# Attention followed by a gated projection, on one core: loads of batch 1 ahead of w_out, the first output by quarters, and the front of batch 2 in its own slot

## The chip, the cores and the metric

The kernel runs on one core of one Trainium2 chip. The metric is device time in microseconds (us), as the median of the runs. The kernel before takes 264.88 us (264.41 to 265.37 in the four runs). Inside the profile the span from the first to the last instruction is about 2 us shorter than the measured time: 263.0 us for the kernel before.

The **granted clock** is the TensorE clock that the throttle allowed, as a share of full speed. A **slot** is one round of the steady state: it computes `h` of one batch while `out` of the batch before fills TensorE's gaps. **T** is the moment at which the matmuls of `s1(2)`, the first attention scores of batch 2, start in the changed kernel. A run's **state** is fast or slow, and only fast runs are compared; here "slow" also covers runs over 1.5% above the fastest run of the same kernel, at an ordinary clock.

## The reference

```python
# q, k, v: [8 batches, 8 heads, 576, 64];  p: [8, 8, 32, 64];  w_in [512, 2048], w_out [2048, 512]
def sm_attn(qq, kk, vv):
    s = scale * (qq @ kk.T);  s = s - max(s)
    a = exp(s);  a = a / (sum(a) + 1e-9)
    return a @ vv
p_packed = sm_attn(p, k, v)               # 32 summary rows for each head
out = sm_attn(q, p_packed, p_packed)
x = out, with the heads side by side      # [8 * 576, 512]
h = x @ w_in
g = h * cos(h)
return g @ w_out                          # [4608, 512] float32
```

## The kernel before

Each batch goes through a chain, its *front*: transpose k; `s1` (p with k, Exp); transpose that result (`a1T`); `pp` (times v); `ppw` (times `w_in`, in four pieces); transpose q; `s2` (q with pp, Exp); `sums2` and `normalise`. Then come `h_mm`, sixteen steps of matmul, cosine on ScalarE and product on VectorE, and `out`, sixteen matmuls for each of its four or five chunks.

Transposes of k, q and a1 are made on TensorE for the first batches (`pe_T`, `a1_pe`) and by DMA later (`xbar`, `a1_xbar`). The DMA transposes and nearly all output stores are issued from the same queue, SyncE's, in program order. Input loads are issued from GpSimd's.

```python
att_pool = ctx.enter_context(tc.tile_pool(name="att", bufs=1))   # kT, qT, a1T: one buffer each
A = ctx.enter_context(tc.tile_pool(name="psA", bufs=3, space=PSUM))
O = ctx.enter_context(tc.tile_pool(name="psO", bufs=2, space=PSUM))

def xbar(n, b):
    t = xT[n, b] = att_pool.tile([128, H * 3, TP], BF16, name=n + "T", tag=n + "T")
    nc.sync.dma_start_transpose(out=t, in_=bf[n, b].rearrange("p h x -> p (h x)"))
def a1_xbar(b): ...                       # the same for a1, on the same queue

# --- loads: all of w_out (2 MB) ahead of batch 1
# ... k 0, v 0, q 0, w_in ...
for n in range(4):
    load_w_out(n)
load("k", 1)
# ... v 1, q 1, k 2, v 2, q 2 ...

# --- first phase: h of batch 0
sums2(0, 0)
sums2(0, 1)
ppw(0, 1)                                 # its copy on ScalarE stands ahead of normalise
normalise(0)
warm(6)                                   # warm-up: matmuls whose result isn't used
dup_p(2, 16)
for fc in range(NFC):
    h_mm(0, fc)()
    # ... ppw(0, 2), ppw(0, 3), pack_p(1, 3) among them ...

# --- fronts of batches 1 AND 2, filled with out of batch 0
# ... s1(1), pp(1), s2(1), k 2 transposed, s1(2), normalise(1), a1_pe(2) ...
load("k", 3)

def slot(s, pieces, hooks): ...           # h of batch s, out of s-1, given pieces of fronts

def begin_loads(b):                       # a "gate": GpSimd reads kT, so it waits for its transpose
    G.tensor_copy(out=gate, in_=xT["k", b][0:1, 0, 0:1])
    for n, i in (("v", b), ("q", b), ("k", b + 1)):
        load(n, i)

xbar("q", 2)
xbar("k", 3)
slot(1, [..., (7, lambda: pp(2)), ...], [(8, lambda: begin_loads(3))])

for s in range(2, B):                     # steady state
    # ... s2(s), fill(8) ...
    s1(s + 1)
    xbar("q", s + 1)
    xbar("k", s + 2)
    a1_xbar(s + 1)
    # ... sums2, normalise, loads of v s+2, q s+2, k s+3 ...
    slot(s, [..., (5, lambda: pp(s + 1)), ...], [])
```

The softmax here doesn't subtract the row's maximum and nothing guards it: scores larger than these inputs give would overflow.

## Time and profile before

| | before |
|---|---|
| time, median of 4 runs | 264.88 us |
| span in the profile | 263.0 us |
| TensorE busy | 93% |
| first cosine of batch 0 | 23.61 us |
| first Exp of `s1(1)` | 41.53 us |
| slot 1 ends, `s2(2)` follows | 75.82 us |
| gate, with the loads of v 3, q 3, k 4 behind it | 68.31 us |
| `pp(3)` starts, without a wait | 91.59 us |
| `s2(3)` starts: slot 2 is over | 106.70 us |

These are from parts 1 and 2 of the page of the kernel before: busy time with its share of the span, then the span in 40 slices of 6.6 us, each digit the busy share (or the granted clock) in tenths.

```profile
PE 244.6 (93%) x2037; PEld 132.1 (50%) x2037; DVE 158.5 (60%) x248; ACT 182.7 (69%) x276; POOL 53.5 (20%) x67
...
PE   8758779998989999999999999999999999999993
...
PEclk9997999999999999999999999999999999999998
```

From slice 13 on, which begins at 79 us, TensorE is busy all the time, so time can be won only before that. The table of busy time by stretches has more detail; its columns are the stretch, its length, then for each engine busy us with its count of instructions, the granted clock, the DMA share, and GB/s.

```profile
core 0: us, PE busy (x) PEld busy (x) DVE busy (x) ACT busy (x) POOL busy (x), PEclk, DMA share, GB/s
...
93.00:101.00 8.00, 8.00 (x62) 4.31 (x61) 6.35 (x9) 5.64 (x10) 0.61 (x1) 1.00 1.22 201
101.00:106.00 5.00, 4.99 (x44) 2.61 (x42) 3.98 (x5) 3.74 (x6) 0.00 (x0) 1.00 0.65 133
```

Both rows lie in slot 2. Here TensorE is busy 12.99 of 13 us.

The timeline of ScalarE around the first cosine shows the delay that the change aims at first: start, duration, engine, line, operation, and in brackets the idle time before it and what ended it.

```profile
17.18 1.25 ACT L200 ACTIVATE lns<-psA 128x576 f32<-128x576 f32 x2
19.93 1.01 ACT L75 CAST PPW<-psA 128x1024 bf16<-128x1024 f32 x1 [1.51 <-PE psA L182]
20.84 1.26 ACT L206 ACTIVATE lns<-lns 128x576 f32<-128x576 f32 x2
22.12 1.28 ACT L225 ACT_TABLE_LOAD   x1
23.61 0.74 ACT L225 ACTIVATE cosT<-psA,pihalf 128x576 bf16<-128x576 f32 x1 [0.21 <-PE psA L221]
```

After the two Ln (L200) ScalarE waits 1.51 us for `ppw(0, 1)`, copies its result (L75), and only then runs the two Exp of `normalise` (L206).

The timeline of SyncE's queue shows the three transposes that slot 2 needs, one behind the other.

```profile
79.21 3.40 SPq L93 DMA_TRANSPOSE qT<-qbf  x1
82.79 2.96 SPq L93 DMA_TRANSPOSE kT<-kbf  x1
85.80 1.57 SPq L147 DMA_TRANSPOSE a1T<-a  x1
```

The duration is the time that the queue was held: the first ends at 82.61 us and the next starts at 82.79, that one ends at 85.75 and the last starts at 85.80. The transpose of a1 lands 3.8 us after its issue, at 89.6 us. `pp(3)`, which needs it, starts at 91.59 us without a wait.

### The profile page before, as it was taken

Reading aid. Unit: us, or ns where it says so; the run is one execution under the profiler, and the core shown is the slowest. Engines: PE = TensorE matmul, PEld = TensorE weight load, DVE = VectorE, ACT = ScalarE, POOL = GpSimd, SP = SyncE. Lnnn points to the kernel's source line nnn. Section 1 sums busy time; section 2 is a strip of 40 time slices with the busy share of each in tenths; the row PEclk is TensorE's granted clock in tenths of the full one; section 3 lists DMA queues with packets and bytes.
Section 4 is the critical chain, followed back from the end, with each engine's and each line's share of the span. In section 5 each row is a group of like instructions: output and inputs, shape, how many; then the busy total and the mean of one; then the engine's idle time right before and its main releaser. Section 6 shows DMA issues by size and latency. Waiting matters only on the chain.

```text
span 263.0 us, 5065 instructions
## 1 busy us (share of the span) xinstructions
PE 244.6 (93%) x2037; PEld 132.1 (50%) x2037; DVE 158.5 (60%) x248; ACT 182.7 (69%) x276; POOL 53.5 (20%) x67
## 2 busy tenths in 40 slices
PE   8758779998989999999999999999999999999993
PEld 3433446455534555456445644464446554565452
DVE  2446886748853787358835685378735873578110
ACT  1358882497698757987798768877897678886000
POOL 8523002440422220504050302220040000000000
PEclk9997999999999999999999999999999999999998
DMA  6999999999399899399949992899194111111232
GB/s 95 203 226 206 206 204 197 192 186 201 47 203 203 189 165 187 73 193 173 221 95 184 168 221 75 159 188 176 47 158 113 40 42 40 40 46 36 80 82 80
DMA packets 62919, 37.09 MB, mean 141 GB/s; under 512 B 35520, under 2 KB 58304, under 8 KB 62896
## 3 DMA queue, kind: packets, MB, share of 16 engines
q0 software_dynamic: 23168, 18.81, 47.1%
q1 hardware_dynamic: 39568, 17.83, 31.5%
q8 instruction: 16, 0.26, 0.4%
q10 hardware_dynamic: 160, 0.13, 0.2%
q14 instruction: 7, 0.06, 0.1%
HBM read 37.22 MB, written 9.44 MB: 177 GB/s over the span
## 4 chain that ended last, share of the span: by engine, by line
PE 66%; DMA 13%; ACT 9%; DVE 7%; issue 2%; POOL 1%; DVEq 0%; ACTq 0%; POOLq 0%
PE ot L271 39%; PE psA L221 17%; DMA kbf<-in_k_dram 7%; DMA w_in_bf<-in_moe_w_in_dram 5%; DVE gT L228 4%; ACT cosT L225 3%; PE psA L182 2%; PE psA L163 2%; DVE PPW L77 2%; ACT PPW L75 1%; ACT L438 1%; PE psA L124 1%; PE ot L260 1%; PE psA L198 1%; PE psA L102 1%
## 5 line engine op out<-in xcount | busy, mean ns | idle before, releaser
L271 PE MATMUL ot<-w_out_bf,gT 128*128 128x512 bf16 x512 | 132.1, 380 | 0.0
L225 ACT ACTIVATE cosT<-psA,pihalf 128x576 bf16<-128x576 f32 x128 | 94.0, 742 | 32.0 <-PE psA L221 30.7
L228 DVE TENSOR_TENSOR gT<-psA,cosT 128x576 bf16<-128x576 f32 x128 | 94.9, 754 | 33.7 <-ACT cosT L225 32.6
L221 PE MATMUL psA<-a2n,PPW 128*128 128x288 bf16 x512 | 83.4, 285 | 5.5 <-DVE gT L228 3.1
L221 PEld LDWEIGHTS <-PPW 128*128 128x128 bf16 x512 | 49.9, 97 | 43.0 <-issue 13.0
L271 PEld LDWEIGHTS <-gT 128*128 128x128 bf16 x512 | 47.0, 98 | 42.8 <-issue 7.1
L232 POOL COPY joint<-gT 128x512 bf16<-128x512 bf16 x16 | 9.7, 614 | 111.1 <-DVE gT L228 111.1
L208 DVE SCALAR_TENSOR_TENSOR a2n<-a2u,r,lns 128x576 bf16<-128x576 bf16 x16 | 12.4, 815 | 20.1 <-ACT lns L206 20.1
L77 DVE COPY osb<-ot 128x512 f32<-128x512 f32 (+1 forms) x19 | 12.7, 670 | 15.1 <-PE ot L271 12.0
L75 ACT COPY osb<-ot 128x512 f32<-128x512 f32 (+1 forms) x18 | 10.3, 574 | 15.0 <-PE ot L271 10.1
L77 DVE CAST PPW<-psA 128x1024 bf16<-128x1024 f32 x16 | 19.5, 1220 | 1.5 <-PE psA L182 1.2
L75 ACT CAST PPW<-psA 128x1024 bf16<-128x1024 f32 x16 | 16.1, 1005 | 2.6 <-PE psA L182 2.6
L77 POOL COPY vp<-vbf 96x3072 bf16<-96x3072 bf16 x6 | 16.5, 2749 | 1.2 <-DMA vbf<-in_v_dram 1.2
L182 PE MATMUL psA<-w_in_bf,ppT 64*32 64x512 bf16 x256 | 13.4, 393 | 2.2 <-DMA w_in_bf<-in_moe_w_in_dram 1.5
L271 PE MATMUL ot<-w_out_bf,joint 128*128 128x512 bf16 x48 | 12.9, 380 | 0.0
L190 ACT ACTIVATE a2u<-psA,rs 128x576 bf16<-128x576 f32 x16 | 11.0, 738 | 2.5 <-PE psA L124 2.4
L200 ACT ACTIVATE lns<-psA 128x576 f32<-128x576 f32 x16 | 10.5, 658 | 2.3 <-PE psA L198 2.3
L133 ACT ACTIVATE a<-psA 128x576 bf16<-128x576 f32 x16 | 10.3, 651 | 2.6 <-PE psA L124 2.6
L173 ACT CAST ppT<-psA 64x128 bf16<-64x128 f32 x16 | 4.2, 260 | 10.8 <-PE psA L102 6.5
L142 DVE RECIPROCAL r<-sums 128x2 f32<-128x2 f32 x8 | 1.3, 160 | 16.5 <-ACT a L133 16.5
L84 POOL DMA_DIRECT2D kbf<-in_k_dram x8 | 6.3, 786 | 21.2 <-PE psA L102 17.3
L320 PE MATMUL wps<-wz 128*128 128x512 bf16 x25 | 9.4, 537 | 1.2 <-DVE wz L342 1.2
(55 smaller groups left out, 152.4 us busy)
## 6 DMA issues: line engine op xcount, KB each, us to landing
kbf<-in_k_dram POOLq DMA_DIRECT2D x8, 576.0 KB, 11.4
vbf<-in_v_dram POOLq DMA_DIRECT2D x8, 576.0 KB, 6.8
qbf<-in_q_dram POOLq DMA_DIRECT2D x8, 576.0 KB, 9.4
out_dram<-osb SPq DMA_DIRECT2D x24, 192.0 KB, 2.8
out_dram<-osb SPq DMA_DIRECT2D x22, 128.0 KB, 2.4
w_in_bf<-in_moe_w_in_dram POOLq DMA_DIRECT2D x4, 512.0 KB, 15.3
w_out_bf<-in_moe_w_out_dram POOLq DMA_DIRECT2D x4, 512.0 KB, 20.2
out_dram<-osb SPq DMA_DIRECT2D x26, 64.0 KB, 2.2
```

Source lines behind the costliest of these rows:

```text
L75: ACT.copy(out=out, in_=in_)
L77: eng.tensor_copy(out=out, in_=in_)
L133: ACT.activation(out=a1[b % 2][:, y, :, 0:TP].rearrange("p (e m) x -> p e m x", e=2), in_=ps[y][:, :, 0:HS].rearrange("p e (m x) -> p e m ...
L182: nc.tensor.matmul(ps[32 * x:32 * x + 32, y, :], ppT[b % 2][r, 2 * x + y, :], w_in_bf[r, x, n * 512:(n + 1) * 512], start=True, stop=True)
L190: ACT.activation(out=a2u[b][:, y].rearrange("p (e x) -> p e x", e=2), in_=ps[y][:, :, 0:HS], func=AF.Exp, scale=rs1[b][:, y:y + 1])
L200: ACT.activation(out=lns[b][:, y].rearrange("p (e x) -> p e x", e=2), in_=ps[:, :, 0:HS], func=AF.Ln)
L208: V.scalar_tensor_tensor(out=a2n[b][:, y], in0=a2u[b][:, y], scalar=r1[b][:, y:y + 1], in1=lns[b][:, y], op0=ALU.mult, op1=ALU.mult)
L221: nc.tensor.matmul(ps[:, e, 0:HS], PPW[b][:, y, fc * 128:(fc + 1) * 128], a2n[b][:, y, e * HS:(e + 1) * HS], start=(y == 0), stop=(y == 1))
L225: ACT.activation(out=csv, in_=ps[:, :, 0:HS], func=AF.Sin, bias=pihalf)
L228: V.tensor_tensor(out=gT[b][:, fc, :].rearrange("p (e x) -> p e x", e=2), in0=ps[:, :, 0:HS], in1=csv, op=ALU.mult)
L232: G.tensor_copy(out=joint[b // 2][:, fc - 7:fc + 1, j0:j0 + 64], in_=gT[b][:, fc - 7:fc + 1, 512:576])
L271: nc.tensor.matmul(ps, w, w_out_bf[:, fc, :], start=(fc == 0), stop=(fc == NFC - 1))
```

## The change

Its intent is to shorten the first 75 us:

1. `ppw(0, 1)` moves behind the first h, so that `normalise` isn't held up by its copy.
2. k 1 and v 1 are loaded ahead of w_out; the first output chunks then follow w_out by quarters, in case it comes late.
3. Every fourth h of batch 0 goes into two half-size buffers of the output's pool, as a fourth h buffer.
4. The front of batch 2 (k 2 on TensorE, `s1(2)`, `a1_pe(2)`, `pp(2)`, `ppw(2, ..)`) moves out of the front of batch 1 and of slot 1, into slot 2.

The diff, cut to its core (it also splits the loads of k 0 and q 0 in two, moves those of p, and takes four warm-up matmuls out: `warm(9)` becomes `warm(7)`, `warm(6)` becomes `warm(4)`):

```diff
 def h_mm(b, fc):
-        ps = psa()
+        if b == 0 and fc % 4 == 3:
+            halves = [O.tile([128, 512], FP32, name="hh", tag="ot") for _ in range(2)]
+            # ... cosine and product then run on each half
+        else:
+            ps = psa()
 # out_gen, batch 0: two chunks in turn, four fc each
+            order = [(c, fc) for n in range(4) for c in range(2) for fc in range(4 * n, 4 * n + 4)] + order[32:]
 # loads
-    for n in range(4):
-        load_w_out(n)
     load("k", 1)
     load("v", 1)
+    load_w_out(0)
     load("q", 1)
+    for n in range(1, 4):
+        load_w_out(n)
 # first phase
-    ppw(0, 1)
     normalise(0)
-    warm(6)
+    warm(4)
     for fc in range(NFC):
         h_mm(0, fc)()
-        if fc in (2, 6):
-            ppw(0, 2 + fc // 4)
+        if fc in (0, 3, 6):
+            ppw(0, 1 + fc // 3)
+        if fc == 8:
+            dup_p(1, 3, V)
+        if fc == 13:
+            pe_T("k", 1, (V, ACT, V))
 # front of batch 1: the pieces of batch 2 go
-    pe_T("k", 2)
-    s1(2)
-    a1_pe(2)
-    recips(2)
-    load("k", 3)
+    xbar("k", 2)
     xbar("q", 2)
+    load("k", 3)
     xbar("k", 3)
-    slot(1, [... pp(2), ppw(2, 0), ppw(2, 1) ...], [(8, lambda: begin_loads(3))])
+    slot(1, [(1, pw(1, 2)), (5, pw(1, 3)), (9, lambda: pack_p(3, B))],
+         [(8, lambda: begin_loads(xT["k", 3], (("v", 3), ("q", 3), ("k", 4))))])
+    # slot 2 is written out: the front of batch 2 first
+    s1(2)
+    permute_v(3)
+    fill(12)
+    a1_pe(2)
+    # ... pp(2), ppw(2, 0), s2(2), ppw(2, 1) with fills ...
+    s1(3)
+    xbar("q", 3)
+    xbar("k", 4)
+    a1_xbar(3)
+    # ... sums2(2, ..), normalise(2), fill(13) ...
+    begin_loads(a1T[3], (("v", 4), ("q", 4), ("k", 5)))
+    slot(2, [(1, pw(2, 2)), (3, pw(2, 3))] + front(3), [])    # front(3) begins with pp(3)
-    for s in range(2, B):
+    for s in range(3, B):
```

`kT` has one buffer. The transpose of k 3 may not overwrite it before `s1(2)` has read k 2, and `s1(2)` now comes after slot 1. The gate still waits for the transpose of k 3.

More of the change, by code (lines that the diff above doesn't have):

```diff
@@ L80, in psa, with load @@
         return A.tile([128, 2, 512 if dt == FP32 else 1024], dt, name="psA", tag="A")
-    def load(n, b):
+    def load(n, b, cuts=(0, 8)):
         bf[n, b] = bf_pool.tile([TP, H, C * D], BF16, name=n + "bf", tag=n + "bf")
-        G.dma_start(out=bf[n, b], in_=srcs[n][b].rearrange("h (p c) d -> p h (c d)", c=C))
+        src = srcs[n][b].rearrange("h (p c) d -> p h (c d)", c=C)
+        for a, z in zip(cuts, cuts[1:]):
+            G.dma_start(out=bf[n, b][:, a:z], in_=src[:, a:z])
     def permute_v(b, eng=G):
@@ L217, in h_mm @@
                 joint[b // 2] = j_pool.tile([128, NFC, 128], BF16, name="joint", tag="joint")
-        ps = psa()
+        if b == 0 and fc % 4 == 3:
+            halves = [O.tile([128, 512], FP32, name="hh", tag="ot") for _ in range(2)]
+            units = [(halves[e][:, 0:HS].rearrange("p (o x) -> p o x", o=1), slice(e, e + 1)) for e in range(2)]
+        else:
+            ps = psa()
+            halves = [ps[:, e, :] for e in range(2)]
+            units = [(ps[:, :, 0:HS], slice(0, 2))]
         for y in range(2):
             for e in range(2):
-                nc.tensor.matmul(ps[:, e, 0:HS], PPW[b][:, y, fc * 128:(fc + 1) * 128],
+                nc.tensor.matmul(halves[e][:, 0:HS], PPW[b][:, y, fc * 128:(fc + 1) * 128],
                                  a2n[b][:, y, e * HS:(e + 1) * HS], start=(y == 0), stop=(y == 1))
@@ L224, in h_mm @@
         csv = cs.rearrange("p (e x) -> p e x", e=2)
-        ACT.activation(out=csv, in_=ps[:, :, 0:HS], func=AF.Sin, bias=pihalf)
+        for sv, es in units:
+            ACT.activation(out=csv[:, es], in_=sv, func=AF.Sin, bias=pihalf)
         def rest():
-            V.tensor_tensor(out=gT[b][:, fc, :].rearrange("p (e x) -> p e x", e=2),
-                            in0=ps[:, :, 0:HS], in1=csv, op=ALU.mult)
+            gv = gT[b][:, fc, :].rearrange("p (e x) -> p e x", e=2)
+            for sv, es in units:
+                V.tensor_tensor(out=gv[:, es], in0=sv, in1=csv[:, es], op=ALU.mult)
             if fc % 8 == 7:
@@ L266, in out_gen @@
     def out_gen(b):
-        for c in range(n_chunks(b)):
-            ps = O.tile([128, DM], FP32, name="ot", tag="ot")
-            for fc in range(NFC):
-                w = joint[b // 2][:, fc, :] if c == 4 else gT[b][:, fc, c * 128:(c + 1) * 128]
-                nc.tensor.matmul(ps, w, w_out_bf[:, fc, :], start=(fc == 0), stop=(fc == NFC - 1))
-                if fc < NFC - 1:
-                    yield
-            osb = o_pool.tile([128, DM], FP32, name="osb")
-            copy((V, ACT)[n_out[0] % 2], osb, ps)
-            n_out[0] += 1
-            for a, z, rows in pieces_of(b, c):
-                nc.sync.dma_start(out=rows, in_=osb[a:z, :])
+        order = [(c, fc) for c in range(n_chunks(b)) for fc in range(NFC)]
+        if b == 0:
+            order = [(c, fc) for n in range(4) for c in range(2) for fc in range(4 * n, 4 * n + 4)] + order[32:]
+        ps = {}
+        for c, fc in order:
+            if fc == 0:
+                ps[c] = O.tile([128, DM], FP32, name="ot", tag="ot")
+            w = joint[b // 2][:, fc, :] if c == 4 else gT[b][:, fc, c * 128:(c + 1) * 128]
+            nc.tensor.matmul(ps[c], w, w_out_bf[:, fc, :], start=(fc == 0), stop=(fc == NFC - 1))
+            if fc == NFC - 1:
+                osb = o_pool.tile([128, DM], FP32, name="osb")
+                copy((V, ACT)[n_out[0] % 2], osb, ps[c])
+                n_out[0] += 1
+                for a, z, rows in pieces_of(b, c):
+                    nc.sync.dma_start(out=rows, in_=osb[a:z, :])
             yield
@@ L300, in load_w_out, with load_p, dup_p @@
                     in_=moe_w_out.rearrange("(a p) n -> p a n", p=128)[:, n * 4:(n + 1) * 4, :])
-    def dup_p(a, b):
+    def load_p(a, b):
+        G.dma_start(out=p_raw[:, 2 * a:2 * b, :], in_=p_rows[:, 2 * a:2 * b, :])
+    def dup_p(a, b, eng):
         for t in range(2):
-            V.tensor_copy(out=p_bf[:, a:b, t, :], in_=p_raw[:, a:b, :])
-    def load_w_in(n):
-        G.dma_start(out=w_in_bf[:, :, n * 512:(n + 1) * 512],
-                    in_=moe_w_in.rearrange("(a p) n -> p a n", p=128)[:, :, n * 512:(n + 1) * 512])
-    def load_w_out(n):
-        G.dma_start(out=w_out_bf[:, n * 4:(n + 1) * 4, :],
-                    in_=moe_w_out.rearrange("(a p) n -> p a n", p=128)[:, n * 4:(n + 1) * 4, :])
-    def dup_p(a, b):
-        for t in range(2):
-            V.tensor_copy(out=p_bf[:, a:b, t, :], in_=p_raw[:, a:b, :])
+            eng.tensor_copy(out=p_bf[:, 2 * a:2 * b, t, :], in_=p_raw[:, 2 * a:2 * b, :])
     def warm(n):
@@ L322 @@
     nc.sync.dma_start(out=p_raw[:, 0:2, :], in_=p_rows[:, 0:2, :])
-    load("k", 0)
+    load("k", 0, (0, 6, 8))
     load("v", 0)
     make_identity(nc, ident)
-    load("q", 0)
-    load_w_in(0)
-    load_w_in(1)
-    G.dma_start(out=p_raw[:, 2:, :], in_=p_rows[:, 2:, :])
-    load_w_in(2)
-    load_w_in(3)
+    load("q", 0, (0, 6, 8))
     for n in range(4):
-        load_w_out(n)
+        load_w_in(n)
+    load_p(1, 3)
     load("k", 1)
     load("v", 1)
+    load_w_out(0)
     load("q", 1)
+    for n in range(1, 4):
+        load_w_out(n)
+    load_p(3, B)
     load("k", 2)
+    load("q", 2)
     load("v", 2)
-    load("q", 2)
     wz = const.tile([128, 512], BF16, name="wz")
@@ L351 @@
     warm(7)
-    dup_p(0, 2)
+    dup_p(0, 1, V)
     pack_p(0, 1)
-    warm(9)
+    warm(7)
     pe_T("k", 0, (V, ACT, V))
@@ L366 @@
     sums2(0, 1)
-    ppw(0, 1)
     normalise(0)
-    warm(6)
-    dup_p(2, 16)
+    warm(4)
     for fc in range(NFC):
         h_mm(0, fc)()
-        if fc in (2, 6):
-            ppw(0, 2 + fc // 4)
-        if fc == 10:
+        if fc in (0, 3, 6):
+            ppw(0, 1 + fc // 3)
+        if fc == 8:
+            dup_p(1, 3, V)
+        if fc == 9:
             pack_p(1, 3)
+        if fc == 13:
+            pe_T("k", 1, (V, ACT, V))
     set_filler(0)
     ACT.preload_act_table_set(EXP_SET)
-    fill(4)
-    pe_T("k", 1)
-    fill(3)
     s1(1)
@@ L387 @@
     recips(1)
-    fill(4)
     pp(1)
     pe_T("q", 1)
-    fill(3)
     ppw(1, 0)
     s2(1)
-    fill(4)
-    pe_T("k", 2)
+    fill(8)
     ppw(1, 1)
-    fill(3)
-    s1(2)
-    fill(4)
     sums2(1, 0)
@@ L403 @@
     normalise(1)
-    fill(6)
-    a1_pe(2)
-    recips(2)
-    load("k", 3)
+    fill(12)
+    dup_p(3, B, G)
+    permute_v(2)
     def slot(s, pieces, hooks):
@@ L422, in pw, with front, begin_loads @@
         return lambda: ppw(b, n)
-    def begin_loads(b):
-        G.tensor_copy(out=gate, in_=xT["k", b][0:1, 0, 0:1])
-        for n, i in (("v", b), ("q", b), ("k", b + 1)):
-            load(n, i)
-    permute_v(2)
+    def front(b):
+        return [(5, lambda: pp(b))] + [(8 + 2 * n, pw(b, n)) for n in range(4)]
+    def begin_loads(t, names):
+        G.tensor_copy(out=gate, in_=t[0:1, 0, 0:1] if len(t.shape) == 3 else t[0:1, 0, 0, 0:1])
+        for n, b in names:
+            if b < B:
+                load(n, b)
+    xbar("k", 2)
     xbar("q", 2)
+    load("k", 3)
     xbar("k", 3)
-    slot(1, [(1, pw(1, 2)), (4, pw(1, 3)), (7, lambda: pp(2)), (9, lambda: pack_p(3, B)),
-             (11, pw(2, 0)), (14, pw(2, 1))], [(8, lambda: begin_loads(3))])
-    for s in range(2, B):
+    slot(1, [(1, pw(1, 2)), (5, pw(1, 3)), (9, lambda: pack_p(3, B))],
+         [(8, lambda: begin_loads(xT["k", 3], (("v", 3), ("q", 3), ("k", 4))))])
+    set_filler(1)
+    ACT.preload_act_table_set(EXP_SET)
+    s1(2)
+    permute_v(3)
+    fill(12)
+    a1_pe(2)
+    recips(2)
+    fill(4)
+    pp(2)
+    fill(5)
+    ppw(2, 0)
+    s2(2)
+    fill(4)
+    ppw(2, 1)
+    s1(3)
+    xbar("q", 3)
+    xbar("k", 4)
+    a1_xbar(3)
+    recips(3)
+    fill(5)
+    sums2(2, 0)
+    fill(5)
+    sums2(2, 1)
+    normalise(2)
+    fill(13)
+    begin_loads(a1T[3], (("v", 4), ("q", 4), ("k", 5)))
+    slot(2, [(1, pw(2, 2)), (3, pw(2, 3))] + front(3), [])
+    fill(1000)
+    for s in range(3, B):
         nxt = s + 1 < B
@@ L449 @@
             recips(s + 1)
-            G.tensor_copy(out=gate, in_=a1T[s + 1][0:1, 0, 0, 0:1])
         fill(4)
@@ L456 @@
         fill(13)
-        for n, b in (("v", s + 2), ("q", s + 2), ("k", s + 3)):
-            if b < B:
-                load(n, b)
-        pieces = [(1, pw(2, 2)), (4, pw(2, 3))] if s == 2 else []
         if nxt:
-            pieces += [(5, lambda: pp(s + 1))] + [(8 + 2 * n, pw(s + 1, n)) for n in range(4)]
-        slot(s, pieces, [])
+            begin_loads(a1T[s + 1], (("v", s + 2), ("q", s + 2), ("k", s + 3)))
+        slot(s, front(s + 1) if nxt else [], [])
         fill(1000)
```

## The prediction

> What bounds it now. TensorE: 93% busy (page, part 1); from 75.8 us to 241 us the table by stretches shows it busy 98 to 100% of every slot, so time is to be won only before 75.8 us. There the timeline shows three stages. (1) 0 to 22.4 us, dependent front of batch 0: TensorE busy 17.0 us, much of it warm-up matmuls; the last delay is ppw(0,1) waiting for w_in until 19.23, and its ScalarE copy (1.01 us) standing ahead of normalise's two Exp. (2) 22.4 to 37.2 us, h of batch 0: ScalarE 12.25 and VectorE 12.95 of 14.8 us busy. (3) 37.2 to 75.8 us: out of batch 0, fronts of batches 1 and 2, h of batch 1. k of batch 1 lands at 39.1, behind 2 MB of w_out (0.86 us wait); slot 1 takes 18.3 us for about 15 us of matmuls.
>
> What the change does.
> (a) ppw(0,1) after the first h: Exp can follow Ln at 18.4 instead of 20.84, so the first cosine starts near 21.2 instead of 23.6: -2.4 us. Splitting k of batch 0 gains nothing: v still lands at about 10.3, and permute_v stands before the a1T copies on VectorE.
> (b) h of batch 0 gets all three remaining ppw, dup_p and pack_p back to back, and the transposes of k 1. The half-bank h costs extra: [...] about +0.15 us on VectorE (estimate from 754 ns at 576 and 1220 ns at 1024). Estimate: the phase grows from 14.6 to about 19 us, and Exp of s1(1) starts at about 41.5 to 42, no earlier than before (41.53).
> (c) The front of batch 1 without the pieces of batch 2: h of batch 1 starts near 54.5 instead of 57.5 us, with 32 out matmuls left instead of 21. Slot 1 has two ppw fewer and becomes TensorE-bound: ends at about 71 instead of 75.8 us. But some 7 us of batch 2's front (s1, a1, pp, two ppw, sums behind 0.2 to 1.2 us copies) moves into slot 2, which without waits would end at 104: -2.8 us.
> (d) New wait. kT has one buffer, so the transpose of k 3 waits for s1(2), which now comes after slot 1. The gate, hence the loads of v 3, q 3, k 4, waits for that transpose: (71 + 0.5 + 4.9) about 76.5 us instead of 68.4. Transposes of q 3, k 4 and a1 3 stand in this order on the queue: k 4 lands about 12 us after the gate, then 3.0 (k) and 3.8 us (a1): a1T of batch 3 lands about 25 us after s1(2). TensorE reaches pp(3) about 21.4 us after s1(2): it stalls about 4 us. Slot 2 then ends at about 108.5 instead of 106.7 us.
> The rest, 156 us, is as before.
>
> Prediction: 266.7 us, 8 in 10 between 262.8 and 270. Chances: faster by over 2% 0.06, within 2% 0.86, slower by over 2% 0.08.
>
> Right or wrong in the profile: first cosine near 21.2 (a); first Exp of s1(1) near 41.5 to 42 (b); w_out never waited for by TensorE; slot 1 ends near 71 (c); pp(3) on TensorE idle 3 to 5 us for a1T by transpose, v 3 issued near 76 (d); from there a constant offset.
>
> What would make it wrong: phase (b) much shorter than my chain by hand, with which slot 1 ends at 69 and the total falls to 264; loads on an otherwise idle queue landing earlier, so no stall (262 to 263); stores held behind the blocked transpose stalling out's buffers (slower).

One term is cut from (b), the extra time on ScalarE of the half-size cosine: it rested on a figure that no run shows. With this term the estimate for the phase came to about 19 us, and the forecast to 266.7 us; both numbers stand as they were made, so what is left of (b) doesn't give the whole growth from 14.6 to 19.

## The result, and the profile after

The changed kernel takes 274.51 us (272.81 to 275.41, four fast runs) against 264.88. The ratio is 1.0356, with a 95% interval of 1.0302 to 1.0410: slower by 3.6%. All ratios in this text are the mean time of one kernel's fast runs over the mean of the other's fast runs of the same rounds, so not quite the ratio of the medians quoted.

The same parts of the page, after:

```profile
PE 245.8 (90%) x2009; PEld 132.8 (49%) x2009; DVE 156.2 (57%) x248; ACT 183.8 (67%) x281; POOL 56.6 (21%) x72
...
PE   8786567989999629999999999999999999999994
...
PEclk9959999999999957999999999999999999999999
```

There is a hole in slices 14 and 15 (89 to 102 us, with slices of 6.8 us), and the clock falls in slices 15 and 16. The stretches around it:

```profile
core 0: us, PE busy (x) PEld busy (x) DVE busy (x) ACT busy (x) POOL busy (x), PEclk, DMA share, GB/s
...
93.00:101.00 8.00, 0.15 (x4) 0.14 (x4) 0.76 (x1) 0.74 (x1) 0.12 (x1) 0.68 1.00 195
101.00:106.00 5.00, 5.00 (x37) 3.04 (x36) 2.09 (x4) 1.26 (x3) 2.36 (x4) 0.50 0.82 135
```

From 93 to 101 us TensorE does 0.15 us of work. From 101 to 106 us it is busy throughout, and that at half clock. The timeline of TensorE names the wait:

```profile
92.39 0.65 PE L229 MATMUL psA<-a2n,PPW 128*128 128x288 bf16 x4
100.89 1.44 PE L165 MATMUL psA<-a1T,vp 96*128 96x64 bf16 x24 [7.85 <-DMA a1T<-a]
102.14 1.04 PE L285 MATMUL ot<-w_out_bf,gT 128*128 128x512 bf16 x2
102.98 1.16 PE L229 MATMUL psA<-a2n,PPW 128*128 128x288 bf16 x4
```

`pp(3)` (L165) waited 7.85 us for the transpose of a1 of batch 3. Compare the first and the last line, both one step of h with four matmuls: 0.65 us ahead of the wait, 1.16 us behind it.

The queue of SyncE, after:

```profile
72.66 3.05 SPq L95 DMA_TRANSPOSE kT<-kbf  x1
75.80 2.92 SPq L291 DMA_DIRECT2D out_dram<-osb  x6
90.00 3.72 SPq L95 DMA_TRANSPOSE qT<-qbf  x1
93.89 3.00 SPq L95 DMA_TRANSPOSE kT<-kbf  x1
96.99 1.48 SPq L149 DMA_TRANSPOSE a1T<-a  x1
```

The transpose of k 3 goes out at 72.66 us, after `s1(2)` at T = 71.94. The six stores that stood behind it go out in a burst of 2.92 us. The gate opens at 77.49 us and the loads start at 78.01. q 3 has landed by 90.00, and the three transposes follow each other: a1 lands 3.77 us after 96.99, at 100.76 us.

The first phase changed too, and its gain is smaller than it was to be:

```profile
18.20 1.28 ACT L202 ACTIVATE lns<-psA 128x576 f32<-128x576 f32 x2
19.38 1.25 ACT L208 ACTIVATE lns<-lns 128x576 f32<-128x576 f32 x2
20.64 1.28 ACT L234 ACT_TABLE_LOAD   x1
22.13 0.74 ACT L234 ACTIVATE cosT<-psA,pihalf 128x576 bf16<-128x576 f32 x1 [0.20 <-PE psA L229]
```

Exp (L208) now follows Ln (L202) at once, but Ln itself starts 1 us later than before. The first cosine is at 22.13 us instead of 23.61. In the same profile the clock of slice 3 is 0.5, in the last line of the page above.

| | before | predicted | after |
|---|---|---|---|
| first cosine | 23.61 | 21.2 | 22.13 |
| first Exp of `s1(1)` | 41.53 | 41.5 to 42 | 41.43 |
| slot 1 ends | 75.82 | 71 | 71.94 |
| gate | 68.31 | 76.5 | 77.49 |
| TensorE reaches `pp(3)`, after T | – | 21.4 | 21.10 |
| wait at `pp(3)` | 0 | 4 | 7.85 |
| `s2(3)` starts | 106.70 | 108.5 | 116.18 |
| from there to the end of the span | 156.3 | as before | 156.7 |

So 9.48 us of the 9.9 us between the two spans are lost by the time `s2(3)` starts, all within slot 2: slot 1 is 3.9 us *ahead* of the kernel before when it ends.

### The profile page after: what moved, and what is told of

The parts are those of the page before. It is cut to its first block, busy times and chain, and to the rows that moved or that the text cites. A ratio compares the mean times of both kernels' runs of the same rounds, so it can differ in the third digit from the quotient of the medians.

```text
span 272.9 us, 5021 instructions
## 1 busy us (share of the span) xinstructions
PE 245.8 (90%) x2009; PEld 132.8 (49%) x2009; DVE 156.2 (57%) x248; ACT 183.8 (67%) x281; POOL 56.6 (21%) x72
## 4 chain that ended last, share of the span: by engine, by line
PE 65%; DVE 13%; ACT 12%; DMA 4%; issue 2%; SPq 1%; POOL 0%; DVEq 0%; ACTq 0%; POOLq 0%
PE ot L285 38%; PE psA L229 17%; DVE gT L239 8%; ACT cosT L234 5%; DMA vbf<-in_v_dram 3%; DVE PPW L77 3%; PE psA L165 3%; PE psA L184 2%; PE psA L200 2%; PE psA L126 2%; ACT L468 1%; DMA a1T<-a 1%; SPq L95 1%; PE ot L270 1%; ACT a2u L192 1%
## 5 line engine op out<-in xcount | busy, mean ns | idle before, releaser
L239 DVE TENSOR_TENSOR gT<-psA,cosT 128x576 bf16<-128x576 f32 x124 | 92.3, 755 | 37.8 <-ACT cosT L234 35.5
L234 ACT ACTIVATE cosT<-psA,pihalf 128x576 bf16<-128x576 f32 x124 | 91.6, 743 | 32.6 <-PE psA L229 31.0
L229 PE MATMUL psA<-a2n,PPW 128*128 128x288 bf16 x496 | 82.3, 288 | 4.5 <-DVE gT L239 1.9
L75 ACT COPY osb<-ot 128x512 f32<-128x512 f32 (+1 forms) x18 | 10.3, 574 | 15.6 <-PE ot L285 10.7
L175 ACT CAST ppT<-psA 64x128 bf16<-64x128 f32 x16 | 4.2, 260 | 21.4 <-DVE ppT L171 17.2
L165 PE MATMUL psA<-a1T,vp 96*128 96x64 bf16 x192 | 7.5, 199 | 9.9 <-DMA a1T<-a 7.9
L165 PEld LDWEIGHTS <-vp 96*128 96x128 bf16 x192 | 7.0, 101 | 11.1 <-issue 10.3
L202 ACT ACTIVATE lns<-psA 128x576 f32<-128x576 f32 x16 | 10.4, 660 | 1.9 <-PE psA L200 1.8
L171 DVE CAST ppT<-psA 64x128 bf16<-64x128 f32 x16 | 4.6, 288 | 11.2 <-PE psA L165 10.9
L86 POOL DMA_DIRECT2D kbf<-in_k_dram x9 | 6.9, 769 | 19.0 <-PE psA L104 12.1
```

The lines of the kernel that those rows point to most:

```text
L75: ACT.copy(out=out, in_=in_)
L165: nc.tensor.matmul(ps[:, 0, hp * 64:(hp + 1) * 64], vp[b][:, c, hp * 128:(hp + 1) * 128], a1T[b][0:TP, :, j, 32 * hp:32 * hp + 32], start= ...
L202: ACT.activation(out=lns[b][:, y].rearrange("p (e x) -> p e x", e=2), in_=ps[:, :, 0:HS], func=AF.Ln)
L229: nc.tensor.matmul(halves[e][:, 0:HS], PPW[b][:, y, fc * 128:(fc + 1) * 128], a2n[b][:, y, e * HS:(e + 1) * HS], start=(y == 0), stop=(y = ...
L234: ACT.activation(out=csv[:, es], in_=sv, func=AF.Sin, bias=pihalf)
L239: V.tensor_tensor(out=gv[:, es], in0=sv, in1=csv[:, es], op=ALU.mult)
```

## The experiments

Fifteen experiments were run, of fourteen different kernels (5 is 2 again), in four groups, each group on one chip with runs of the kernel before among them (its medians were 265.11, 264.79, 265.17 and 264.98 us). The changed kernel itself wasn't run again in these groups, so what an experiment wins against it is read across groups. The theory: the lost time is (1) the wait for a1T, longer than predicted because of late loads and of three transposes in series; and (2) a half clock that follows the wait. The rivals: the cost lies in the changed order of the work itself, in the fourth h buffer, in the single kT buffer alone, or in the clock of the first phase.

Most of the kernels are read by the same moments of slot 2; a table at the end of this section collects them.

### 1. a1 ahead in the queue

```diff
     s1(3)
+    a1_xbar(3)
     xbar("q", 3)
     xbar("k", 4)
-    a1_xbar(3)
```

> The changed kernel with one transpose moved: a1T of batch 3 is issued ahead of the transposes of q 3 and k 4. Nothing else. Theory A (the 7.85 us idle of TensorE before pp(3), plus half clock after it, is the loss): a1T lands near 86 us instead of 100.8, pp(3) follows at about 93 us without a wait, no granted-clock dip after it, slot 2 ends near 105 instead of 116.2 us, time about 263.5 us (0.995 of before). Rival B (moving the front of batch 2 into its own slot costs TensorE time of itself): time stays above 268 us without any wait at pp(3).

It ran at 269.86 us (267.35 to 270.61), ratio 1.0161 (1.0095 to 1.0227). That wins 4.7 us of the 9.6, and the wait shrinks to 2.15 us without going. The reason is in the trace, in the instructions of the line that transposes a1:

```profile
L149 SPq DMA_TRANSPOSE a1T<-a x1: 4215/4215/4215, 83.5 to 83.5; - x1
...
DMA to landing us min/median/max: 12.0/12.0/12.0
```

Issued at 83.46 us, while the loads of v 3, q 3 and k 4 were under way, the transpose landed after 12.0 us. In the changed kernel, where those loads were over, it took 3.8 us. The clock fell behind this wait too, to a mean of 0.79 from 93 to 101 us and back to 1.00 from 101 to 106.

### 2. v 3 and q 3 loaded without the gate

Their buffers are free at this point of slot 1; only k 4 has to wait for the transpose of k 3.

```diff
-         [(8, lambda: begin_loads(xT["k", 3], (("v", 3), ("q", 3), ("k", 4))))])
+         [(8, lambda: (load("v", 3), load("q", 3), begin_loads(xT["k", 3], (("k", 4),))))])
```

> The changed kernel, with v 3 and q 3 loaded at fc 8 of slot 1 without the gate on the transpose of k 3; only k 4 stays behind the gate. Theory A with late loads as its cause: v 3 and q 3 issue near 66 us and land before 77, transpose of q 3 is issued near 80 instead of 90.0 us, k 4 lands near 85, a1T near 92 us: no wait at pp(3), or under 1 us; time about 264 us. If instead the order of the transposes alone matters (k 4 lands at 92.8 as now) the stall stays over 6 us.

Three fast runs gave 265.78 to 268.43 us, ratio 1.0065 (1.0013 to 1.0116). The same kernel was run again in the next group, as experiment 5.

### 3. Two kT buffers

```diff
+    kT_pool = ctx.enter_context(tc.tile_pool(name="kTp", bufs=2))
-        t = xT[n, b] = att_pool.tile(...)
+        t = xT[n, b] = (kT_pool if n == "k" else att_pool).tile(...)
```

> The changed kernel with two buffers for kT, so that the transpose of k 3 no longer waits for s1(2). If the single kT buffer is the whole cause of the late loads (as the prediction put it): v 3 is issued at 68 to 70 us as before, the stall goes, time about 264. If the load of k 3, issued at 62.9 and landed at 70.6 us because it waits for the transpose of k 2, is nearly as late: the gate opens only near 76, stall 5.5 to 6.5 us, time 271 to 273 us.

271.68 us (270.99 to 272.40), ratio 1.0245 (1.0217 to 1.0274): 2.8 us won. The transpose of k 3 doesn't wait for `s1(2)` any more, but the gate opens only 0.7 us earlier (76.82), because k 3 itself lands at about 71.9: its load stands behind `permute_v(2)` on GpSimd and needs the buffer of k 2, whose transpose stands behind the first stores in SyncE's queue. The loads after the gate came faster (v 3 in 6.5 us, against 9.1), and the wait was 3.57 us. The single buffer, which the prediction named as *the* cause, is thus only one of several things that hold the gate at this time.

### 4. The wait kept, the clock kept up

Thirty-six idle matmuls stand ahead of `pp(3)`, so that TensorE is busy during the wait.

```diff
+    def idle_work():
+        t = psa()
+        for _ in range(36):
+            nc.tensor.matmul(t[:, 0, :], wz[:, 0:128], wz, start=True, stop=True)
-    slot(2, [(1, pw(2, 2)), (3, pw(2, 3))] + front(3), [])
+    slot(2, [(1, pw(2, 2)), (3, pw(2, 3)), (5, idle_work)] + front(3), [])
```

> The changed kernel with 36 idle matmuls of 512 columns (7.7 us, result unused) put just before pp(3), where TensorE now sits idle for 7.85 us. The loads and a1T come no earlier (a1T still lands near 100.8 us). If the idle time lowers the granted clock and this costs 2 to 3 us after pp(3): clock stays 1.00 from 93 to 106 us, slot 2 ends near 113.7 instead of 116.2 us, time about 272 us, below the changed kernel by 2 to 3 us. If the half clock costs nothing: time 274.5 as before the edit, or longer.

As a time this missed: 276.76 us (273.32 to 277.25), ratio 1.0409, no faster than the change itself. As a measurement it answered. First two lines of TensorE's timeline (the trace holds 35 of the 36 matmuls), then one stretch of the table of busy times:

```profile
97.67 7.93 PE L465 MATMUL psA<-wz 128*128 128x512 bf16 x35
...
105.44 0.86 PE L165 MATMUL psA<-a1T,vp 96*128 96x64 bf16 x24
```

```profile
101.00:106.00 5.00, 4.95 (x41) 2.53 (x41) 0.00 (x0) 0.00 (x0) 2.48 (x4) 1.00 0.71 124
```

The clock stays at 1.00 from 101 to 106 us, and `pp(3)` takes 0.86 us instead of 1.44. From `pp(3)` to `s2(3)` (118.48) it is 13.04 us, against 15.29 in the changed kernel. The half clock therefore costs 2.25 us. The time didn't fall, because the idle matmuls started late and ran past the wait they were to fill (a1T had landed at 101.0 us, 4.4 us before `pp(3)` started): TensorE had already lost 2.44 us earlier, to a product on VectorE that took 3.3 us instead of 0.82. Experiments 10 and 15 return to that one.

### 5 to 8. Parts of the first phase, on top of experiment 2

The base is experiment 2 again. Each of the others differs from it by one thing: 10 more warm-up matmuls (6), `dup_p(1, 3)` moved from h step 8 to step 5 so that `pack_p` needn't wait (7), and no fourth h buffer (8).

```diff
 # 6
-    warm(7)                                 # after pack_p(0, 1)
+    warm(9)
     a1_pe(0)
+    warm(5)
-    warm(4)                                 # after normalise(0)
+    warm(7)
 # 7
-        if fc == 8:
+        if fc == 5:
             dup_p(1, 3, V)
 # 8
-        if b == 0 and fc % 4 == 3:
+        if False:
```

> The kernel of e2_loads_early once more, because its only profile fell into a slow execution (clock 0.75) and the other three of this call are edits of it. Theory A2 (without the stall the change is worth nothing, because slot 2 carries what slot 1 shed and the first 40 us gain little): a1T of batch 3 lands before TensorE needs it, slot 2 ends at 105 to 107 us (before: 106.7), time 265.5 to 267, within 1% of before. If theory A alone held (the prediction's 104.6 us end of slot 2 without the stall): 262.5 to 263.5 us.

> e5 plus 10 warm-up matmuls: 9 for 7 ahead of the transposes of k 0, 5 new ones after a1_pe(0), where TensorE idles 1.3 us for a1T, 7 for 4 after normalise(0). If the granted clock of 0.52 between 14 and 21 us (before: 0.87) is what made the first cosine come at 22.1 and not 21.2 us: clock over 0.9 there, first cosine near 21.3, time 0.5 to 1.5 us under e5. If not, no difference or longer.

> e5 with dup_p(1, 3) after the sixth h instead of the ninth. The 2.08 us that TensorE waits for p_bf ahead of pack_p in the first phase goes (under 0.3 us). If that wait is on the way: first Exp of s1(1) 1 to 2 us earlier, time 1 to 2 us under e5. If the two copying engines set the pace of that phase anyway: under 0.5 us.

> e5 without the fourth h buffer: all h of batch 0 in the three psA buffers. The half tiles cost about 0.15 us on ScalarE and 0.05 us on VectorE each (0.89 and 0.81 us the pair against 0.74 and 0.76 whole). If the fourth buffer hides bubbles: the first phase gets 1 to 2 us longer, time 1 to 2 us over e5. If the phase is paced by ScalarE and VectorE: within 0.7 us of e5.

| | fast runs, us | ratio to before (95%) |
|---|---|---|
| 5, base | 265.37 to 268.77 (4 runs) | 1.0076 (1.0038 to 1.0113) |
| 6, more warm-up | 267.93 to 268.73 (4) | 1.0135 (1.0117 to 1.0152) |
| 7, dup early | 264.81 to 268.31 (4) | 1.0067 (1.0025 to 1.0109) |
| 8, three h buffers | 265.33 to 268.84 (4) | 1.0066 (1.0026 to 1.0106) |

Runs of the base, of 7 and of 8 scatter over more than 3 us, where the kernel before stays within about 1 us, so nothing under about 0.4% can be told here. The fourth h buffer is worth nothing that these runs can show. In its profile the more-warm kernel did what was intended, with the clock at 1.00 from 0 to 42 us and the first cosine at 21.65; still its times are no better; its wait at `pp(3)` (2.12 us), with the lower clock behind it (a mean of 0.87 from 93 to 106 us), remained. That it is even slower than the base is not explained by these runs, and it hangs on which runs count: two of six runs each of 5, 7 and 8 were over the 1.5% line and are left out, and with its two (270.91 and 272.22 us) the base's mean would be 268.5 us, the same as that of 6. The base's profile shows a wait of 2.57 us at `pp(3)`, where the transpose of q 3 took 9.8 us to land beside the load of k 4.

### 9 and 12. Both kT buffers, and k 2 and k 3 handled early

```diff
 # 9, on top of experiment 3
     normalise(1)
+    xbar("k", 2)                            # ahead of the first stores
     fill(12)
     dup_p(3, B, G)
+    load("k", 3)
     permute_v(2)
-    xbar("k", 2)
     xbar("q", 2)
-    load("k", 3)
     xbar("k", 3)
 # 12 = 9 with dup_p(1, 3) at h step 5
```

> The changed kernel with the whole chain of k 3 moved ahead: two kT buffers, the transpose of k 2 issued ahead of the first stores, k 3 loaded ahead of permute_v(2). The front of batch 2 stays in its own slot. Theory (the stall is the late chain k 2 transpose, k 3 load, k 3 transpose, gate, loads; nothing else in slot 2 is wrong): transpose of k 2 issued near 48 us, gate near 66, v 3 issued near 66.5 as before, k 4 lands before 80, a1T near 90 us, TensorE reaches pp(3) near 93 without a wait and without a clock dip, slot 2 ends at 105 to 106, time 263 to 265 us, clear of before by less than 1%. If the stall stays over 2 us, the chain is not the cause.

> e9 with dup_p(1, 3) after the sixth h as in e7, whose profile was in a slow execution. If the 2.1 us wait ahead of pack_p in the first phase is on the way: 1 to 2 us under e9, about 262 to 263 us, which would beat both kernels. If the phase is paced by ScalarE and VectorE: within 0.7 us of e9.

Experiment 9: five fast runs of 266.81 to 269.91 us, ratio 1.0128 (1.0093 to 1.0163), without a sixth of 278.54; experiment 12: 269.59 (267.88 to 270.81), ratio 1.0168 (1.0131 to 1.0205). Against experiment 3 they win over 1% and about 0.8%, but the 263 to 265 us expected of 9 were missed. Here too a transpose met loads: that of k 2, now issued beside the loads of q 2 and v 2, took 10.9 us to land, where those of k took 4.9 to 5.2 us in the kernel before. The gate came at 72.89 us in experiment 9, against 76.82 in experiment 3. Moving dup_p early brought nothing on top.

### 10. The stores not held back

The transpose of k 3 and the gated loads move behind `s1(2)` in the program, so that stores of slot 1 needn't stand behind a blocked transpose.

```diff
     load("k", 3)
-    xbar("k", 3)
-    slot(1, [...], [(8, lambda: begin_loads(xT["k", 3], (("v", 3), ("q", 3), ("k", 4))))])
+    slot(1, [...], [])
     # ...
     s1(2)
+    xbar("k", 3)
+    begin_loads(xT["k", 3], (("v", 3), ("q", 3), ("k", 4)))
     permute_v(3)
```

> The changed kernel with the transpose of k 3 and the gated loads placed behind s1(2) in the program, so that they no longer stand ahead of the stores of batch 0 on their queues; they wait for the same thing as before. If the six stores that burst out at 75.8 us made v 3 take 9.1 us to land (6.5 in e3): stores go out from 66 us on, v 3 lands in about 6.5 us, transpose of q 3 near 87.5 instead of 90.0, stall near 5 instead of 7.85 us, time 271.5 to 272.5. If not: stall 7.5 to 8.5 us, time as the changed kernel (274.5).

274.18 us (272.38 to 275.33), ratio 1.0339 (1.0303 to 1.0375), no different from the change. Yet the part that was to change did. These are the DMA issues of the stretch behind the gate, first of the changed kernel, then of this one; the columns end with size and median us to landing.

```profile
vbf<-in_v_dram POOLq DMA_DIRECT2D x1, 576.0 KB, 9.1
qbf<-in_q_dram POOLq DMA_DIRECT2D x1, 576.0 KB, 11.2
kbf<-in_k_dram POOLq DMA_DIRECT2D x1, 576.0 KB, 13.3
```

```profile
vbf<-in_v_dram POOLq DMA_DIRECT2D x1, 576.0 KB, 6.4
qbf<-in_q_dram POOLq DMA_DIRECT2D x1, 576.0 KB, 8.5
kbf<-in_k_dram POOLq DMA_DIRECT2D x1, 576.0 KB, 10.8
```

Without the burst of six stores, the loads land 2.5 to 2.7 us sooner. How much of that is the burst isn't settled: experiment 15, with its stores free too, gives 6.4, 8.5 and 10.7 us, but experiment 4, with the same burst as the changed kernel, gives 7.7, 9.8 and 12.0. With the burst the loads of these profiles landed between 1.2 and 2.7 us later. The gate in its turn opened later (T + 6.75 us, against T + 5.55), and a1T landed 27.3 us after T, against 28.8.

But the loads that came sooner started something else sooner. v 3 had landed, so GpSimd began `permute_v(3)` at 86.82 us, while VectorE was at the first of the two products of `normalise(2)`. Here is the line of VectorE's timeline:

```profile
86.32 4.03 DVE L210 SCALAR_TENSOR_TENSOR a2n<-a2u,r,lns 128x576 bf16<-128x576 bf16 x2 [1.77 <-ACT lns L208]
```

Two products took 4.03 us; they take 1.55 us otherwise. TensorE waited 2.43 us for them. That delay and the remaining wait at `pp(3)` (2.62 us) add up to 5.05 us; the clock fell behind both (0.63 and 0.67 in the two us after each).

### 15. As 10, with `permute_v(3)` held until the products are done

```diff
 # on top of experiment 10
     begin_loads(xT["k", 3], (("v", 3), ("q", 3), ("k", 4)))
-    permute_v(3)
     # ...
     normalise(2)
+    G.tensor_copy(out=gate, in_=a2n[2][0:1, 1, 0:1])
+    permute_v(3)
     fill(13)
```

> e10 with permute_v(3) held on GpSimd until a2n of batch 2 is written. In e10 (and e4) the second a2n took 3.3 us instead of 0.82, in the very stretch in which GpSimd copied v (86.8 to 89.7 us), and TensorE waited 2.4 us for it. If the two copies disturb each other: both a2n take 0.82 us and that wait goes; a1T, which sets the end, lands when it did in e10 (100.5 us), so the time stays within 1.5 us of it. If the long a2n has another cause, it stays 3.3 us.

One run, so of unknown state: 272.18 us. The same line of VectorE's timeline:

```profile
85.06 1.55 DVE L210 SCALAR_TENSOR_TENSOR a2n<-a2u,r,lns 128x576 bf16<-128x576 bf16 x2 [1.77 <-ACT lns L208]
```

The products are back at 1.55 us, and TensorE's wait for them is gone. The copy on GpSimd was the cause: in experiment 10 it ran from 86.82 to 89.74 us, beside the second product, which took 3.3 us; here it starts at 86.86 us, when both products are done (86.61), and the second took 0.82 us. By what means the copy holds a product up, these runs don't show. TensorE then reaches `pp(3)` earlier and waits there for longer (6.41 us), as it should where a1T comes at a fixed time (T + 27.4).

### 11. The first part of the change alone, in the kernel before

```diff
     sums2(0, 1)
-    ppw(0, 1)
     normalise(0)
     ...
         h_mm(0, fc)()
+        if fc == 0:
+            ppw(0, 1)
```

> The kernel before, with one part of the change alone: ppw(0, 1) after the first h instead of ahead of normalise. Prediction of this part: first cosine 2.4 us earlier. If the earlier start reaches the end: time 1.5 to 2.4 us under before (ratio 0.991 to 0.994). If k of batch 1, which lands at 39.1 us behind w_out, or the pace of the first phase holds it back: within 0.5 us of before.

265.55 us (264.57 to 266.65), ratio 1.0021 (0.9993 to 1.0048): no gain. The first cosine comes 2.56 us earlier, at 21.05 us. The end of the phase then meets the load of k 1: TensorE waits for it for 2.22 us, where it waited 0.86 us before, and starts the transposes of k 1 at the same moment (39.05 and 39.11 us). In the kernel before, the gain is bounded by the load, which is a reason for the change to have moved that load.

### 13 and 14. No wait, and then no low clock either

Experiment 13 joins 1 and 2, and lets the next gate wait for the transpose of k 4 instead of a1T, so that it is the last one in the queue as before. Experiment 14 adds 6 and 7.

```diff
 # 13, on top of experiment 2
     s1(3)
+    a1_xbar(3)
     xbar("q", 3)
     xbar("k", 4)
-    a1_xbar(3)
     # ...
-    begin_loads(a1T[3], (("v", 4), ("q", 4), ("k", 5)))
+    begin_loads(xT["k", 4], (("v", 4), ("q", 4), ("k", 5)))
 # 14 = 13 with the warm-ups of 6 and the dup_p of 7
```

> e2 (v 3 and q 3 loaded early) and e1 (a1T of batch 3 transposed first) together, the next loads gated on the transpose of k 4 so that no load runs beside the transposes. The first version that should have no wait at pp(3) at all. a1T issued near 83.5 with the queue quiet, landed by 88 us (3.8 us, not 12.0 as in e1). Theory A (stall and clock are the whole loss, the change itself worth about 1 to 2 us): slot 2 ends near 105.3 us, time 262.5 to 264. Rival A2 (without the stall the change is worth nothing): slot 2 ends at 106 to 107.5, time 264.5 to 266.5.

> e13 with the 10 more warm-up matmuls of e6 and dup_p(1, 3) early as in e7: the best of what the runs so far suggest. If the clock dips and the 2.1 us wait of the first phase are on the way: 1 to 2 us under e13, about 262 us, under before by 1%. If not: within 0.7 us of e13.

Experiment 13 ran at 265.85 us (264.72 to 266.83), ratio 1.0035 (1.0013 to 1.0057). `pp(3)` waits for nothing; a1T, issued at 83.97 us when v 3 and q 3 had landed, took 4.5 us. Of the 9.6 us that the change lost, 8.7 are back. The time and the end of slot 2 (106.85 us) are those of rival A2 in its expectation, not of theory A: without the wait the change is worth nothing, but it no longer costs much. What it still lacks is seen in the page's clock row, in slices 3, 4 and 7:

```profile
PE   7587578889999999999999999999999999999993
...
PEclk9958998999999999999999999999999999999999
```

T is 72.88 us here. Experiment 14 has a full clock throughout, and no wait for `p_bf` (2.08 us in 13, gone in 14):

```profile
PE   8876667989999999999999999999999999999993
...
PEclk9999999999999999999999999999999999999999
```

It ran at 263.92 us (263.15 to 265.03), ratio 0.9974 (0.9957 to 0.9991). That is the best kernel and it beats both, by a quarter of a per cent over the kernel before: a difference that the interval bears out, but one of 0.7 us by the ratio (0.0026 of 265). T is 70.26 us, `s2(3)` starts at 104.23 us against 106.70 before. Not all of these 2.47 us reach the end: from there the span has 157.2 us left, against 156.3, and the profiled run is the fastest of the six.

### The same moments, kernel by kernel

All times are us from the start of the span, from TensorE's timeline of each profile of a fast run (15: one run, unknown state). Experiments 2, 7 and 8 are missing because slow runs were profiled, 11 because it is an edit of the kernel before.

| | T | wait at `pp(3)` | `pp(3)` | `pp(3)` to `s2(3)` | `s2(3)` |
|---|---|---|---|---|---|
| after | 71.94 | 7.85 | 100.89 | 15.29 | 116.18 |
| 1, a1 first | 72.36 | 2.15 | 95.61 | 14.61 | 110.22 |
| 3, two kT | 73.89 | 3.57 | 98.55 | 14.49 | 113.04 |
| 4, wait filled | 73.01 | filled | 105.44 | 13.04 | 118.48 |
| 5, loads early | 71.83 | 2.57 | 95.50 | 14.56 | 110.06 |
| 6, more warm-up | 71.46 | 2.12 | 94.67 | 14.60 | 109.27 |
| 9, k early | 72.35 | 1.94 | 95.38 | 13.02 | 108.40 |
| 10, stores free | 73.09 | 2.62 | 100.51 | 14.60 | 115.11 |
| 12, k early, dup | 71.43 | 3.21 | 95.91 | 14.41 | 110.32 |
| 13, no wait | 72.88 | 0 | 93.81 | 13.04 | 106.85 |
| 14, no wait, warm | 70.26 | 0 | 91.19 | 13.04 | 104.23 |
| 15, permute held | 71.83 | 6.41 | 99.32 | 14.40 | 113.72 |

The fifth column is the same work in each of them. It takes 13.0 us where the wait was 0, was filled, or was 1.94 us. It takes 14.4 to 15.3 us where the wait was 2.12 us or more. Two classes, with nothing between. But the length of a wait doesn't decide alone. In the first phase of the changed kernel TensorE waits 2.08 us for `p_bf`, and the clock stays at 1.00 from 29 to 39 us. Experiment 11 has a wait of 2.22 us, longer than those of 1 and 6, and its page shows a full clock throughout:

```profile
39.05 1.19 PE L102 MATMUL psA<-ident,kbf 96*128 96x96 bf16 x24 [2.22 <-DMA kbf<-in_k_dram]
...
PEclk9999999999999999999999999999999999999999
```

## Why the prediction was wrong

The prediction said 266.7 us, within 262.8 to 270; the time is 274.51. Its direction of argument holds, and one of its steps failed: (d) mis-sized one term of its sum and left another out.

**(a) held in the mechanism, not in the size, and reached less far than was thought.** Exp follows Ln directly. The first cosine came at 22.13 us, not 21.2. The clock of this stretch goes with it: where it was 1.00 from 14 to 21 us (6, 9 and 14), the first cosine came at 21.09 to 21.65 us; where it was 0.50 to 0.58 (after, 1, 3, 10 and 13), at 22.09 to 22.90. Two of the change's own edits had taken four warm-up matmuls out. That this lowered the clock isn't shown: experiment 9 has no more of them than the changed kernel, and its clock was full there. Experiment 11 shows that in the kernel before this gain doesn't reach the end at all.

**(b) held.** The first Exp of `s1(1)` came at 41.43 us, against 41.5 to 42 predicted. TensorE waited for no quarter of w_out. The half-size cosine took 0.49 to 0.52 us in the trace; the two of a tile overlap and take 0.89 us together, so the extra over a whole one (0.74) is 0.15 us. The fourth h buffer that this pays for had no effect that could be measured (8 against 5).

**(c) held for slot 1,** which ended at 71.94 us against 71 predicted. For slot 2 "which without waits would end at 104" is about right as well: experiment 14 ends it at 104.23. That is partly luck: slot 2 lasted 33.97 us in 13 and in 14 alike, not 33 (104 - 71), and T was 70.26, not 71. And it took a full clock and an earlier dup_p to get there. Experiment 13, without the wait alone, ends it at 106.85 us, no earlier than the kernel before. So even without the wait, the change as written gains nothing.

**(d) is the step that failed: "it stalls about 4 us. Slot 2 then ends at about 108.5".** It named the right wait, on the right tile, at the right place. But slot 2 ended at 116.18 us, 7.7 us later. The terms of that sum:

| term | predicted | measured | adds |
|---|---|---|---|
| T | 71 | 71.94 | +0.9 |
| T to TensorE at `pp(3)` | 21.4 | 21.10 | -0.3 |
| wait at `pp(3)` | 4 | 7.85 | +3.9 |
| `pp(3)` to `s2(3)`, full clock | 12.1 (108.5 - 71 - 21.4 - 4) | 13.04 (4, 13, 14) | +0.9 |
| half clock behind the wait | not in the sum | 15.29 - 13.04 | +2.3 |

The two large terms are 6.1 of the 7.7 us. The length of slot 2 says the same: 44.24 us in the changed kernel (116.18 - 71.94), 33.97 in experiments 13 and 14, where nothing waits at `pp(3)`. Of the 10.27 us between them, the wait is 7.85 and the half clock 2.25.

*The wait.* The chain of the prediction was: gate, 12 us until k 4 has landed, 3.0 us for its transpose, 3.8 us for that of a1. In the changed kernel the gate opened at 77.49 and k 4 was issued at 79.53 us, for a landing 13.3 us later: 15.3 us behind the gate, not 12. Of these 3.3 us, 2.1 could have been read in the trace of the kernel before. There the gate was at 68.31 and k 4 issued at 69.96 us, landing 12.5 us later, so 14.1 us behind the gate; the prediction seems to have taken the time from *issue* to landing for the time from the *gate*. Of the remaining 1.2 us, 0.4 lie between gate and issue (2.04 us against 1.65) and 0.8 between issue and landing, where the burst of stores fell. Then the transpose of q 3, which the prediction let vanish behind the landing of k 4, ended at about 93.9 us, when k 4 had been there for 1.1 us. (Together these are 4.4 us and not 3.9, because the prediction's chain adds up to 24.3 us from T to a1T, which it called 25.) Experiment 10 frees the stores: the loads land 2.5 to 2.7 us sooner (1.2 to 1.3 against experiment 4), and a1T lands 1.5 us sooner after T. The prediction did name held-back stores among what would make it wrong, but as a stall of the output's buffers. TensorE didn't wait for an output buffer there; what harm the stores did, they did when they were let go.

*The clock.* The granted clock fell in this wait of 7.85 us, and that wasn't in the sum. TensorE fell idle at 93.04 us; the clock was 1.00 until 95, 0.92 from 95 to 96 and 0.50 from 96 us on, and it stayed there for some 5 us of work, until about 106 (0.96 from 106 to 107). Experiment 4 shows the cost as 2.25 us and that with TensorE kept busy the clock is 1.00 from 101 to 106 us. A wait of 4 us, as predicted, would probably have cost clock too: waits of 3.21 and 3.57 us (12 and 3) were followed by 14.41 and 14.49 us for the work of 13.04, so an estimate from these two is about 1.4 us, which was missing from the sum whatever the length of the wait.

What stays open. The changed kernels scatter over 1 to 4 us within the fast state, with mean clocks from 0.96 to 1.00, where the kernel before has 0.98 to 1.00; the dips lie in the first 42 us in the profiles of 13 and 9, but which wait starts each of them wasn't isolated. Nor was it found why experiment 6 isn't faster than 5. And in experiment 14 the shares of warm-up and of dup_p weren't taken apart.

## What to carry to other kernels

When a piece of work moves later, follow every buffer that it reads to the transfer that wants to overwrite it, and from there along the *whole queue* that carries that transfer: here one late reader of kT held back a gate, six stores, three loads and three transposes. Measure such a chain from the event that opens it, and add every issue and every predecessor in the queue. And where the sum gives TensorE a wait of 2 us or more, reckon with a slow clock behind it. At `pp(3)` it cost 1.4 to 2.3 us behind every wait from 2.12 us up; a wait of 2.22 us in experiment 11 cost no clock, so it is a risk and not a rule.

## What the runs showed of the hardware

- **A DMA transpose beside ordinary loads was slow in three runs.** a1T landed after 12.0 us beside three loads (experiment 1) and after 3.8 us without them (after); k 2 after 10.9 us (9), with 4.9 to 5.2 for k in the kernel before; q 3 after 9.8 us (5), with 5.1 in the changed kernel. It need not be: in 13, a1T took 4.5 us with the load of k 4 under way.
- **A blocked transpose held the stores behind it, and their burst seems to slow the loads.** Six stores let go at once went along with loads landing after 9.1, 11.2 and 13.3 us (after) and 7.7, 9.8 and 12.0 us (4); with the stores free it was 6.4, 8.5 and 10.8 us (10).
- **The idle time that costs the clock.** In these profiles waits of 2.12, 2.15 and 2.57 us were followed by the longer time (14.4 to 14.6 us for the work of 13.0), a wait of 1.94 us was not (its clock is 1.00 from 76 us on, in 9), nor did the clock fall behind one of 2.22 us (11). What makes the difference isn't shown; waits of 2.1 us can already cost the clock in this kernel.
- **The table load.** It took 1.28 us, and at the first cosine the trace shows no further delay on either side of it: in the kernel before, the load follows Exp at once (22.12 us) and ends at 23.40, and the cosine behind it starts at 23.61 us, after 0.21 us of waiting for TensorE.
- **VectorE beside GpSimd.** A product of `normalise(2)` took 3.3 us beside a copy of 2.9 us on GpSimd, and 0.82 us without it (10, 15).
